# Low halves of the split numbers formed on VectorE, the cosine's whole turns taken on ScalarE, attention's outputs emptied at once, and the dense weights' conversion let in from head pair 5

## The chip, the cores and the metric

One core of one Trainium2 chip. The metric is the device time of one launch in microseconds (us); less is better. TensorE (PE) multiplies matrices, VectorE (DVE) and ScalarE (ACT) work elementwise from SBUF or PSUM, GpSimd (POOL) does so too and issues the indirect DMAs, SyncE (SP) issues the plain loads.

## What is computed

Three layers behind one another, all inputs and outputs in fp32.

```python
kv = einsum('bhsd,bhse->bhde', k, v); out = einsum('bhsd,bhde->bhse', q, kv)      # 8 x 8 x 576 x 64
x = out / sqrt(mean(out * out, -1) + 1e-6) * g_norm                               # -> x: 4608 x 512
logits = x @ w_gate                              # 8 experts, 576 tokens each, greedy by descending logit
out[tokens of e] = relu(x @ w1[e]) @ w2[e]       # 512 -> 1024 -> 512
h = out @ w_in; g = h * cos(h); result = g @ w_out      # 512 -> 2048 -> 512
```

## The kernel before

The two MLPs run in fp16 on TensorE, each number as a high half and a low half (`hi = fp16(x*s)`, `lo = fp16(x*s - hi)`), so that every product takes three matmuls (`mm3`).

**Attention** walks over 16 head pairs n (4 groups s of 4 pairs). For each, `kv_mm` forms k^T v in PSUM tile P, `kw_t` and `kw_mm` append the 8 gate columns, `tr` transposes q, and `o_mm` multiplies, in three parts g = 0, 1, 2, into PSUM tile pO (two buffers). pO holds groups of 64 output columns and 8 gate columns. `o_mm` empties it: ACT squares it (sq), ACT copies the 64-column blocks (xs), DVE copies the gate columns (LR) and sums the squares (SS). `norm(n)` runs for each pair and puts small DVE steps, one ACT square root and one POOL multiply (xs by R) on a list `late`, of which a few are issued at a time; after a group's last pair the rows go to DRAM (x_rows, from POOL's queue, 2304 KB a group). Loads of k, v, q run three pairs ahead on SP's queue.

**Conversion of the dense weights** (w_in, then w_out; `dense` and `dense_parts`) is background work in 8 parts of 4 units of 512 KB. A unit is loaded by SP into one of three io buffers, ACT rescales its high words (dG), and DVE merges it with three integer instructions into a staging tile (stA or stB, which alternate by part). Behind the fourth unit ACT takes the squares' sum of both tiles (junk), DVE and PE make the scale s (psm, psb, the matmul pq, peb, s), POOL multiplies each tile by s in place, ACT rounds it into the high half (win0 or wout0), and POOL subtracts into the low half. In attention this may run only after pair 13 (`if n > 13: side()`).

**Routing** (`Router.phase`, 8 phases) is a serial chain of small DVE steps and small matmuls (cmp, cn, nS, ...); phase 0 stands alone between attention and the MLPs, the others are woven in.

**Experts and the dense MLP** run over 16 units u of 288 tokens: h (w1), y (w2), then `yfin` (scale and split of y), o (the output product of the unit before, tiles of 128 tokens) and g (w_in with the cosine, `h2`). Weights of expert n are loaded by POOL's queue and split in `split_w` (expert 0 in `first_w`): ACT multiplies, ACT rounds, POOL subtracts. Unit 0's g may not start before the last part of w_in is converted (`flush("bg", ("in", 3))`) and unit 1's o not before the last part of w_out (`flush("bg", ("out", 3))`).

**The cosine** in `h2`, for 8 steps fp of 24 matmuls into one of three PSUM buffers ph: ACT writes r = p*s + 0.25 (et), DVE rounds it by adding and subtracting 1.5 * 2^23 (ek), DVE subtracts (et), ACT takes the sine (et), DVE multiplies by p (eg), ACT rounds (gT, first tile) and POOL subtracts (gT, second tile). The product of step fp is issued after the subtraction of step fp + 1, and the buffer ph is free after it.

The order on every engine is fixed when the kernel is built: `Meter` keeps a modelled clock for each engine, and `Sched` lets background jobs in where the modelled engine would be idle, by slack tables (`SLE`, `SLACK`, `PA`). So a changed cost also moves other instructions.

Of the kernel before, what the change touches and what calls it, by code (L numbers as in the profile page):

```python
# [19 lines left out]
E = 8  # L20
# [8 lines left out]
RB = 9  # L29
NHP = H // 2  # L30


def attention(nc, tc, q, k, v, w_gate, xrows, ident, gcol, L, M, sc):


    with ExitStack() as st:
# [5 lines left out]
        T = {}  # L42

# [19 lines left out]
        KV = [one.tile([128, 2, NHP, 2, D + E], F32, name=f"KV{i}") for i in range(2)]  # L63
# [3 lines left out]
        late = []  # L67
# [7 lines left out]
        def kv_of(n):  # L75

            return KV[n // NHP % 2][:, :, n % NHP]

        def kv_mm(n):
# [12 lines left out]
            for X in range(2):  # L92
                nc.scalar.activation(kv_of(n)[half[X], X, :, 0:D], P[half[X], :, 0:D], AF.Copy)
            for X in (1, 0):
                nc.vector.tensor_copy(kv_of(n)[half[1 - X], X, :, 0:D], P[half[X], :, 0:D])

        def kw_t(n):
            p = ps.tile([128, 4, 128], F32, name="pT", bufs=2)
            for X in range(2):
                for a in range(2):  # L100
                    nc.tensor.matmul(p[64 * a:64 * a + 64, X, 0:D], kv_of(n)[0:64, X, a, 0:D], ident[0:64, 0:64],
                                     start=True, stop=True)
            kvt[n] = wk.tile([128, 2, D], F32, name="kvt")
            nc.scalar.activation(kvt[n], p[:, 0:2, 0:D], AF.Copy)

        def kw_mm(n):
# [6 lines left out]
            nc.vector.tensor_copy(kv_of(n)[:, :, :, D:D + E], p[:, 0:2, 0:2 * E].rearrange("p x (a e) -> p x a e", a=2))  # L113
# [21 lines left out]
        def o_mm(n, g):  # L135
            s, hp = divmod(n, NHP)
            if hp == 0 and g == 0:
                XS[s] = wk.tile([128, RB, H, D], F32, name="xs", bufs=2)
# [4 lines left out]
            for j in range(J):  # L143
                for a in range(2):
                    o = (D + E) * (2 * j + a)
                    for X in range(2):
                        for i in range(N):
                            h = slice(64 * i, 64 * i + 64)
                            nc.tensor.matmul(pO[64 * X:64 * X + 64, i, o:o + D + E],
                                             qT[h, 2 * j + X, 64 * a:64 * a + 64], kv[h, X, a, :], start=True, stop=True)  # L150
            po = pO[:, 0:N, 0:2 * J * (D + E)].rearrange("p i (j a e) -> p i j a e", j=J, a=2)
            hs = slice(2 * hp, 2 * hp + 2)

            def rows(x):
                if g == 2:
                    return [x[:, 8, hs]]
                return [x[:, 4 * g + i:4 * g + 4:2, hs] for i in range(2)]

            sq = wk.tile([128, 2, 4, D], F32, name="sq", bufs=2)
            nc.scalar.activation(sq[:, 0:N, 0:2 * J], pO[:, 0:N, 0:2 * J * (D + E)].rearrange("p i (j e) -> p i j e", e=D + E)[:, :, :, 0:D], AF.Square)  # L160
            for i, x in enumerate(rows(XS[s])):
                nc.scalar.activation(x, po[:, i, 0, :, 0:D] if g == 2 else po[:, i, :, :, 0:D], AF.Copy)
# [7 lines left out]
            if g == 2:  # L170
                norm(n)

        def norm(n):
            s, hp = divmod(n, NHP)
            c, hs = slice(RB * s, RB * s + RB), slice(2 * hp, 2 * hp + 2)
            a = wk.tile([128, RB, 2], F32, name="na")
            y = wk.tile([128, RB, 2], F32, name="ny")
            w = wk.tile([128, RB, 2], F32, name="nw")
            x = XS[s][:, :, hs, :]

            def store():
                nc.gpsimd.dma_start(dview(xrows, 2 * s * S * DM, [[RB * DM, 128], [1, RB * DM]]),
                                    XS[s].rearrange("p r h e -> p (r h e)"))

            def logits():
                m = wk.tile([128, RB, H, E], F32, name="lm", bufs=1)
                nc.vector.tensor_mul(m, LR[s], R[:, c, :, None].to_broadcast([128, RB, H, E]))
                late.insert(0, lambda: nc.vector.tensor_reduce(L[:, c, :], m.rearrange("p r h e -> p r e h"), axis=AX,
                                                               op=OP.add))

            late.extend([
                lambda: nc.vector.tensor_scalar(a, SS[:, c, hs], 1.0 / D, 1e-6, op0=OP.mult, op1=OP.add),
# [15 lines left out]
        for n in range(NP + 1):  # L208
# [280 lines left out]
MF = 1.0  # L489
# [198 lines left out]
class Sched:  # L688
# [9 lines left out]
    def __init__(self, meter):  # L698
# [8 lines left out]
        self.held = None  # L707

# [74 lines left out]
    def step(self, name, force=False):  # L783
# [16 lines left out]
        if not force and (job.ready > now + self.early - MF * (name == "fin") or any(c[e] > now + self.slack[e] for e in job.need)):  # L800
# [51 lines left out]
class Moe:  # L852

    def __init__(self, nc, tc, pers, sm, C, xrows, w1, w2, w_in, w_out, out, gcol):
# [11 lines left out]
        nc.vector.memset(self.qtr, 0.25)  # L866
        self.win = [t([128, 4, FF], F16, f"win{i}") for i in range(2)]
        self.wout = [t([128, 16, DM], F16, f"wout{i}") for i in range(2)]
# [81 lines left out]
    def split_far(self, x, s, hi, lo):  # L950
# [613 lines left out]
```

## Time and profile before

| | |
|---|---|
| median of 3 runs | 1550.81 us (1546.31 to 1557.15) |
| profiled execution | 1557.92 us, its span 1556.1 us |
| mean granted TensorE clock | 0.927 of full |
| busy: PE, DVE, ACT, POOL | 88%, 54%, 43%, 37% of the span |

How to read it: a busy share is an average over stages with different limits, so the stages are looked at one by one: attention (0 to 145.4 us), routing phase 0 and the first gathers (to 202.6), the first h, y and h (to 268.2), the first g (to 306.3), y of unit 1 (to 323.8), a stretch with almost no matmul (to 359.7), o of unit 0 (to 389.8), and the rest to 1547.5. In a row of the timeline the last bracket is the idle time of the engine before the instruction and who ended it.

### The profile page before, as it was taken

The page shows a single profiled execution, that of the slowest core. Times are in us where ns is not written, and L with a number is a line of the kernel's source. Part 1 is how long each engine was busy: PE and PEld are TensorE (multiplying, and loading weights), DVE is VectorE, ACT ScalarE, POOL GpSimd, SP SyncE. Part 2 cuts the span into 40 slices and gives each one's busy share as a digit, 9 for nine tenths or more (in the row PEclk, how much of TensorE's full clock was granted, in tenths as well). Part 3 has the DMA queues.
Part 4 walks back from the last instruction along what each step waited for, and adds up shares of the span by engine and source line. Part 5 has one row for each costly group of instructions (what it writes and reads, how often), then busy time and mean ns, then how long its engine had stood idle before and what let it go on. Part 6 is the DMA issues. An engine that isn't in the chain of part 4 may idle for free.

```text
span 1556.1 us, 29014 instructions
## 1 busy us (share of the span) xinstructions
PE 1364.8 (88%) x12072; PEld 918.4 (59%) x12072; DVE 838.4 (54%) x2081; ACT 672.8 (43%) x1133; POOL 573.7 (37%) x493
## 2 busy tenths in 40 slices
PE   6775368726999889998999899999999999999997
PEld 5664236512667556474757466667675757576763
DVE  3567887974766576656655762434243415343441
ACT  3454364634734452055505650366066506642230
POOL 0333463476733342037403640256037203531121
PEclk8786569867999999999999989999999999999999
DMA  7784622322220220003100210021003000200000
GB/s 263 287 286 152 213 94 82 109 67 82 75 76 14 65 68 21 19 4 98 60 8 8 92 62 8 15 96 62 10 5 125 29 21 1 82 1 15 1 14 21
DMA packets 40371, 109.35 MB, mean 70 GB/s; under 512 B 4272, under 2 KB 12464, under 8 KB 39728
## 3 DMA queue, kind: packets, MB, share of 16 engines
q0 software_dynamic: 15744, 62.40, 11.7%
q1 hardware_dynamic: 23808, 45.09, 8.7%
q8 instruction: 94, 1.54, 0.4%
q14 instruction: 37, 0.30, 0.1%
q10 hardware_dynamic: 688, 0.02, 0.0%
HBM read 88.62 MB, written 18.87 MB: 69 GB/s over the span
## 4 chain that ended last, share of the span: by engine, by line
PE 64%; DVE 10%; ACT 5%; POOL 5%; issue 3%; DMA 1%; POOLq 0%; DVEq 0%; ACTq 0%
PE ph L666 61%; PE pr L666 2%; ACT w1s L666 1%; DVE eg L666 1%; POOL stB L666 1%; POOL w2s L666 1%; POOL stA L666 1%; ACT stA L666 1%; ACT et L666 1%; PE pq L666 1%; DVE stB L666 1%; DMA out_dram<-eg,idx 1%; ACT junk L666 1%; ACT xT L666 1%; DVE cmp L666 1%
## 5 line engine op out<-in xcount | busy, mean ns | idle before, releaser
L666 PE MATMUL ph<-wout,gT 128*128 128x512 f16 x1728 | 400.8, 385 | 10.6 <-ACT wout L666 4.5
L666 PE MATMUL ph<-yT,win 128*128 128x288 f16 x3072 | 392.2, 288 | 16.1 <-DVE eg L666 13.7
L666 PEld LDWEIGHTS <-win 128*128 128x128 f16 x3072 | 300.1, 98 | 103.5 <-issue 21.9
L666 PEld LDWEIGHTS <-gT 128*128 128x128 f16 x1728 | 163.2, 99 | 210.0 <-issue 22.2
L666 POOL TENSOR_TENSOR gT<-eg,gT 128x576 f16<-128x576 f32 (+2 forms) x192 | 182.0, 963 | 262.4 <-ACT gT L666 261.7
L666 ACT ACTIVATE et<-ph,qtr,us 128x576 f32<-128x576 f32 x128 | 106.2, 831 | 345.2 <-PE ph L666 315.0
L666 PE MATMUL ph<-xT,w1s 128*128 128x288 f16 x1536 | 206.8, 294 | 17.5 <-DVE hT L666 8.3
L666 PE MATMUL ph<-hT,w2s 128*128 128x288 f16 x1536 | 204.7, 289 | 0.0
L666 PEld LDWEIGHTS <-w1s 128*128 128x128 f16 x1536 | 150.2, 100 | 62.4 <-issue 10.5
L666 POOL DMA_INDIRECT out_dram<-eg,idx x36 | 36.1, 1002 | 402.5 <-DVE scT L666 190.9
L666 PEld LDWEIGHTS <-w2s 128*128 128x128 f16 x1536 | 147.4, 99 | 38.2 <-issue 0.7
L666 DVE TENSOR_SCALAR ek<-et 128x576 f32<-128x576 f32 x128 | 63.3, 494 | 151.9 <-ACT et L666 151.7
L666 DVE SCALAR_TENSOR_TENSOR eg<-ph,cG,et 128x576 f32<-128x576 f32 x128 | 103.9, 812 | 10.7 <-POOL gT L666 5.3
L666 DVE TENSOR_TENSOR eg<-ph,scT 128x512 f32<-128x512 f32 x36 | 24.9, 691 | 150.1 <-PE ph L666 128.9
L666 DVE TENSOR_TENSOR et<-et,ek 128x576 f32<-128x576 f32 x128 | 98.3, 768 | 4.4
L666 ACT ACTIVATE gT<-eg 128x576 f16<-128x576 f32 (+2 forms) x192 | 92.2, 512 | 14.5 <-DVE eg L666 13.9
L666 ACT ACTIVATE et<-et 128x576 f32<-128x576 f32 x128 | 86.3, 674 | 4.8 <-DVE et L666 4.2
L666 DVE SCALAR_TENSOR_TENSOR hT<-ph,hT 128x576 f16<-128x576 f32 x64 | 48.1, 755 | 67.3 <-ACT hT L666 67.1
L666 ACT ACTIVATE yT<-ph,sy 128x576 f16<-128x576 f32 x32 | 22.0, 737 | 138.8 <-DVE sy L666 138.8
L666 ACT ACTIVATE hT<-ph 128x576 f16<-128x576 f32 x64 | 41.0, 646 | 85.4 <-PE ph L666 85.4
L666 POOL TENSOR_TENSOR xs<-xs,R 128x1152 f32<-128x1152 f32 x16 | 36.1, 2254 | 112.0 <-DVE R L666 82.3
L666 DVE TENSOR_REDUCE amy<-ph 128x1 f32<-128x576 f32 x32 | 24.1, 755 | 56.7 <-PE ph L666 56.6
(216 smaller groups left out, 1626.3 us busy)
## 6 DMA issues: line engine op xcount, KB each, us to landing
kt<-in_k_dram SPq DMA_DIRECT2D x16, 576.0 KB, 4.8
vt<-in_v_dram SPq DMA_DIRECT2D x16, 576.0 KB, 6.9
qt<-in_q_dram SPq DMA_DIRECT2D x16, 576.0 KB, 7.4
x_rows<-xs POOLq DMA_DIRECT2D x4, 2304.0 KB, 9.9
io<-in_moe_w_in_dram SPq DMA_DIRECT2D x16, 512.0 KB, 4.8
io<-in_moe_w_out_dram SPq DMA_DIRECT2D x16, 512.0 KB, 3.6
out_dram<-eg,idx POOLq DMA_INDIRECT x36, 2.8
io<-x_rows,idx POOLq DMA_INDIRECT x35, 3.6
```

Source lines behind the costliest of these rows:

```text
L666: return f(*a, **kw)
```

## The change

Six things. (1) Attention: the layout of kv becomes gates, columns, columns, gates for a pair of heads, so that one ACT instruction takes 4 x 128 output columns and one DVE instruction all gates; sums of squares are one reduction; `norm` runs once for each group of 4 pairs; the stores of groups 1 and 2 wait for pair 13; group 1's rows lie in wout's space. (2) The dense conversion may be issued from pair 5 on, with loads granted one by one (`GRANT`). (3) Dense low halves: ACT rounds straight from the staging tile with the scale, DVE forms the low half; POOL does nothing. (4) The same for the experts' weights. (5) Cosine: ACT writes k = int32(p*s + 0.25), DVE forms r = p*s - k, ACT takes sin(2 pi r + pi/2); the low half of the result is formed on DVE. (6) Slacks in `SLE` are set anew.

```diff
+LOADED = 13
+GRANT = {5: 1, 7: 1, 9: 1, 11: 1, 12: 2, 13: 99}
...
+            sq = wk.tile([128, 4, 2, D], F32, name="sq", bufs=2)
+            sqv = sq[:, 0].rearrange("p a e -> p (a e)") if g == 2 else sq.rearrange("p (j i) a e -> p j i (a e)", i=2)
+            nc.scalar.activation(sqv, po[..., E:E + 2 * D], AF.Square)
+            nc.scalar.activation(rows(XS[s]), po[..., E:E + 2 * D], AF.Copy)
             later()
-            for i, x in enumerate(rows(LR[s])):
-                nc.vector.tensor_copy(x, po[:, i, 0, :, D:D + E] if g == 2 else po[:, i, :, :, D:D + E])
-            for i, x in enumerate(rows(SS[:, RB * s:RB * s + RB])):
-                y = sq[:, i, 0:2 * J].rearrange("p (j a) e -> p j a e", a=2)
-                nc.vector.tensor_reduce(x, y[:, 0] if g == 2 else y, axis=AX, op=OP.add)
+            nc.vector.tensor_copy(lrows(LR[s]), gates(po))
+            nc.vector.tensor_reduce(srows(SS[:, RB * s:RB * s + RB]), sq[:, 0] if g == 2 else sq, axis=AX, op=OP.add)
             later()
-            if g == 2:
-                norm(n)
+            if g == 2 and hp == NHP - 1:
+                norm(s)
...
+            M.grant += GRANT.get(n, 0)
             for f in steps:
                 f()
-                if n > 13:
+                if n == LOADED:
+                    while held:
+                        held.pop(0)()
+                    HOLD.clear()
+                if n > 4:
                     side()
...
-            if len(raw) == min(len(units), used + 3) or not self.far and nc.moved > sc.now() + FX:
+            if len(raw) == min(len(units), used + 3, self.grant):
                 return
...
         def low(lo, x, hi, t):
-            yield "gpsimd", 2.08, t
-            nc.gpsimd.tensor_sub(lo, x, hi)
+            yield "vector", 1.2, t
+            nc.vector.scalar_tensor_tensor(lo, x, s, hi, op0=OP.mult, op1=OP.subtract)
...
-            yield "gpsimd", 2.08, t
-            nc.gpsimd.tensor_scalar(x, x, s, None, op0=OP.mult)
-            yield "scalar", 0.95, nc.last
-            nc.scalar.activation(hi, x, AF.Copy)
+            yield "scalar", 1.04, t
+            nc.scalar.activation(hi, x, AF.Identity, scale=s)
...
-            yield from self.split_far(x, s[:, 0:1], hi, lo)
+            self.nc.scalar.activation(hi, x, AF.Identity, scale=s[:, 0:1])
+            yield "result"
+            self.nc.vector.scalar_tensor_tensor(lo, x, s[:, 0:1], hi, op0=OP.mult, op1=OP.subtract)
...
+            k = wk.tile([128, 2, U], I32, name="ek", bufs=1)
+            nc.scalar.activation(k, p, AF.Identity, bias=self.quarter[:, 0:1], scale=s(2))
+            if last:
+                sine(*last)
+            if done:
+                high(*done)
             r = wk.tile([128, 2, U], F32, name="et")
-            nc.scalar.activation(r, p, AF.Identity, bias=self.qtr[:, 0:1], scale=s(2))
-            k = wk.tile([128, 2, U], F32, name="ek", bufs=1)
-            V.tensor_scalar(k, r, MAGIC, MAGIC, op0=OP.add, op1=OP.subtract)
+            V.scalar_tensor_tensor(r, p, s(2), k, op0=OP.mult, op1=OP.subtract)
...
-    E0, E1, H, Y, O = ((2.2, 1.25, 3.24), (1.93, 1.88, 6.34), (0.9, 2.0, 15.0), (2, 4.86, 8.62), (2, 3.96, 20))
+    E0, E1, H, Y, O = ((3, 3, 3.24), (3, 3, 6.34), (3, 3, 15.0), (3, 4, 8.62), (3, 4, 20))
```

What the change moves in the fixed order is shown at three places.

VectorE behind y of unit 1, where the last parts of w_out are converted (dG, io and stB belong to a unit's merge; psm, psb, peb and s4 to a part's scale; numbers tell tiles apart). Before:

```order
L666 SCALAR_TENSOR_TENSOR stB_4516<-io_4504,stB_4516 128x512
L666 TENSOR_REDUCE psm_4537<-am_4382 128x1
L666 TENSOR_SCALAR psb_4539<-psm_4537 128x1
L666 TENSOR_SCALAR peb_4543<-pq_4541 128x1
L666 TENSOR_SCALAR stB_4517<-dG_4535 128x512
L666 TENSOR_SCALAR s4_105<-peb_4543 128x1
L666 SCALAR_TENSOR_TENSOR stB_4517<-dG_4535,stB_4517 128x512
L666 SCALAR_TENSOR_TENSOR stB_4517<-io_4513,stB_4517 128x512
```

Now:

```order
L689 TENSOR_SCALAR s4_106<-peb_4249 128x1
L689 SCALAR_TENSOR_TENSOR stB_4215<-io_4118,stB_4215 128x512
L689 TENSOR_SCALAR stB_4215<-dG_4220 128x512
L689 SCALAR_TENSOR_TENSOR stB_4215<-dG_4220,stB_4215 128x512
L689 SCALAR_TENSOR_TENSOR wout_104<-stA_3868,s4_106,wout_104 128x8x128
L689 SCALAR_TENSOR_TENSOR stB_4215<-io_4137,stB_4215 128x512
L689 TENSOR_SCALAR stB_4216<-dG_4256 128x512
L689 SCALAR_TENSOR_TENSOR wout_104<-stA_3869,s4_106,wout_104 128x8x128
```

Before, the scale of part 2 (s4) stands between the merges of part 3, and eight merges follow the end of y; now four do, and the two low halves of part 2 stand between them.

GpSimd at the same place. Before (a multiply in place, then the low half):

```order
L666 TENSOR_SCALAR stA_4380<-stA_4380,s4_105 128x1024
L666 TENSOR_SCALAR stA_4381<-stA_4381,s4_105 128x1024
L666 TENSOR_TENSOR wout1_103<-stA_4380,wout0_102 128x8x128
L666 TENSOR_TENSOR wout1_103<-stA_4381,wout0_102 128x8x128
L666 TENSOR_SCALAR stB_4516<-stB_4516,s4_105 128x1024
L666 TENSOR_SCALAR stB_4517<-stB_4517,s4_105 128x1024
L666 TENSOR_TENSOR wout1_103<-stB_4516,wout0_102 128x8x128
L666 TENSOR_TENSOR wout1_103<-stB_4517,wout0_102 128x8x128
```

Now, from attention's end to the loads of expert 1, it holds multiplies of attention's rows and DMA issues only:

```order
L689 TENSOR_TENSOR xs_1939<-xs_1939,R_148 128x9x128 x4
L689 DMA x_rows<-xs_1939 128x4608
L689 DMA sti_2899<-in_moe_w1_dram,wi_2894 128x1024
L689 DMA sti_2901<-in_moe_w1_dram,wi_2894 128x1024
L689 DMA sti_2903<-in_moe_w1_dram,wi_2894 128x1024
```

All elementwise work on weights has left GpSimd; the four multiplies of attention's last group now stand together at its end.

VectorE in the cosine, two steps of a later unit. Before:

```order
L666 TENSOR_SCALAR ek<-et 128x576
L666 TENSOR_TENSOR et<-et,ek 128x576
L666 SCALAR_TENSOR_TENSOR eg<-ph,cG,et 128x576
L666 CAST cn<-pr 32x60
L666 TENSOR_SCALAR ek<-et 128x576
L666 TENSOR_TENSOR et<-et,ek 128x576
```

Now:

```order
L689 SCALAR_TENSOR_TENSOR et<-ph,us,ek 128x576
L689 SCALAR_TENSOR_TENSOR eg<-ph,cG,et 128x576
L689 TENSOR_TENSOR gT_3313<-eg,gT_3312 128x2x192
L689 TENSOR_TENSOR gT_3313<-eg,gT_3312 128x2x96
L689 SCALAR_TENSOR_TENSOR et<-ph,us,ek 128x576
```

The rounding and its subtraction have become one instruction that reads PSUM, and the low half, in one or two pieces, stands behind the product.

## Rows read from the trace of the kernel before

**Rows 1.** Windows by stage: length, busy us PE, PEld, DVE, ACT, POOL (instructions), clock, DMA.

```profile
145.40:202.60 57.20, 15.43 (x350) 12.67 (x350) 48.13 (x132) 18.60 (x31) 28.06 (x19) 0.50 0.56 192
202.60:268.20 65.60, 49.33 (x357) 33.85 (x358) 49.77 (x102) 35.39 (x53) 27.93 (x12) 0.83 0.26 81
268.20:306.30 38.10, 27.44 (x219) 20.11 (x218) 36.08 (x63) 21.87 (x32) 17.45 (x9) 0.87 0.32 97
323.80:359.70 35.90, 0.53 (x4) 0.31 (x3) 21.34 (x50) 14.43 (x22) 25.50 (x10) 0.55 0.23 73
359.70:389.80 30.10, 26.79 (x155) 11.65 (x155) 16.68 (x63) 13.31 (x18) 17.49 (x14) 0.85 0.33 105
389.80:656.00 266.20, 251.34 (x1971) 162.42 (x1970) 175.21 (x450) 111.83 (x174) 100.40 (x96) 0.97 0.15 49
656.00:1513.30 857.30, 838.03 (x6032) 565.23 (x6031) 395.13 (x871) 374.53 (x573) 300.90 (x288) 0.99 0.11 37
```

**Rows 2.** Waits, 202.6 to 360 us: total, times, longest.

```profile
PE pq L666 <- DVE psb L666: 31.5, 5, 15.7
...
PE ph L666 <- DVE eg L666: 8.8, 1, 8.8
```

**Rows 3.** Timeline, 329 to 360 us: start, duration, engine, operation.

```profile
329.14 6.51 POOL L666 TENSOR_SCALAR stB<-stB,s 128x1024 f32<-128x1024 f32 x2 [5.47 <-DVE s L666]
...
335.62 4.38 POOL L666 TENSOR_TENSOR wout<-stB,wout 128x1024 f16<-128x1024 f32 x2
...
341.66 0.42 DVE L666 TENSOR_SCALAR stB<-dG 128x512 int32<-128x512 int32 x1
...
342.84 0.69 DVE L666 SCALAR_TENSOR_TENSOR stB<-io,stB 128x512 int32<-128x512 int32 x1
...
353.45 1.06 ACT L666 ACTIVATE junk<-stB 128x1024 bf16<-128x1024 f32 x1
...
358.63 1.06 ACT L666 ACTIVATE wout<-stB 128x1024 f16<-128x1024 f32 x1 [4.03 <-POOL stB L666]
359.74 0.58 PE L666 MATMUL ph<-wout,gT 128*128 128x512 f16 x1 [4.54 <-ACT wout L666]
```

**Rows 4.** Timeline in the first g, 274 to 282 us.

```profile
274.65 4.83 POOL L666 TENSOR_TENSOR win<-stB,win 128x1024 f16<-128x1024 f32 x2
...
277.54 2.49 DVE L666 SCALAR_TENSOR_TENSOR stA<-io,stA 128x512 int32<-128x512 int32 x1
...
281.06 1.55 ACT L666 ACTIVATE et<-ph,qtr,us 128x576 f32<-128x576 f32 x2 [4.71 <-issue]
```

**Rows 5.** Timeline, 195 to 210 us: two low halves of w1 on VectorE.

```profile
195.94 5.94 DVE L666 SCALAR_TENSOR_TENSOR w1s<-sti,sg,w1s 128x1024 f16<-128x1024 f32 x1 [1.33 <-ACT w1s L666]
196.56 4.23 POOL L666 TENSOR_TENSOR win<-stA,win 128x1024 f16<-128x1024 f32 x2
...
208.83 1.28 DVE L666 SCALAR_TENSOR_TENSOR w1s<-sti,sg,w1s 128x1024 f16<-128x1024 f32 x1
```

**Rows 6.** The page's groups of the cosine: count, busy us, mean ns, idle before.

```profile
L666 PE MATMUL ph<-yT,win 128*128 128x288 f16 x3072 | 392.2, 288 | 16.1 <-DVE eg L666 13.7
...
L666 ACT ACTIVATE et<-ph,qtr,us 128x576 f32<-128x576 f32 x128 | 106.2, 831 | 345.2 <-PE ph L666 315.0
...
L666 DVE TENSOR_SCALAR ek<-et 128x576 f32<-128x576 f32 x128 | 63.3, 494 | 151.9 <-ACT et L666 151.7
L666 DVE SCALAR_TENSOR_TENSOR eg<-ph,cG,et 128x576 f32<-128x576 f32 x128 | 103.9, 812 | 10.7 <-POOL gT L666 5.3
...
L666 DVE TENSOR_TENSOR et<-et,ek 128x576 f32<-128x576 f32 x128 | 98.3, 768 | 4.4
...
L666 DVE SCALAR_TENSOR_TENSOR hT<-ph,hT 128x576 f16<-128x576 f32 x64 | 48.1, 755 | 67.3 <-ACT hT L666 67.1
```

**Rows 7.** Groups of ScalarE in attention, 8 to 146 us, by form.

```profile
L666 ACT ACTIVATE xs<-pO 128x256 f32<-128x256 f32 x64 | 21.0, 385 | 0.0
L666 ACT ACTIVATE sq<-pO 128x512 f32<-128x512 f32 x32 | 19.1, 598 | 20.5 <-PE pO L666 20.3
```

More of the change, by code (lines that the diff above doesn't have):

```diff
@@ L62, in attention @@
             nc.vector.tensor_scalar(wgb[r, :, a, :], wgr[r], gcol[r], None, op0=OP.mult)
-        KV = [one.tile([128, 2, NHP, 2, D + E], F32, name=f"KV{i}") for i in range(2)]
+        W2 = 2 * (D + E)
+        KV = [one.tile([128, 2, NHP, W2], F32, name=f"KV{i}") for i in range(2)]
         SS = one.tile([128, NCOL, H], F32, name="SS")
@@ L66, in attention @@
         kvt, qTs, XS, LR = {}, {}, {}, {}
-        late = []
+        late, held = [], []
         M.prf = lambda: ps.tile([128, 4, 128], F32, name="pT", bufs=2).rearrange("p a b -> p (a b)")
@@ L152, in o_mm @@
             hs = slice(2 * hp, 2 * hp + 2)
-            def rows(x):
-                if g == 2:
[L156 to L162, printed above, removed]
@@ L181, in store, with norm, scaled @@
+            later()
+            if g == 2 and hp == NHP - 1:
+                norm(s)
+        def norm(s):
+            c = slice(RB * s, RB * s + RB)
+            a, y, w = (wk.tile([128, RB, H], F32, name=nm, bufs=1) for nm in ("na", "ny", "nw"))
+            x = XS[s]
+            m = LR[s]
+            def scaled(i):
+                h = slice(2 * i, 2 * i + 2)
+                nc.gpsimd.tensor_mul(x[:, :, h], x[:, :, h], R[:, c, h, None].to_broadcast([128, RB, 2, D]))
             def store():
@@ L182, in store @@
                 nc.gpsimd.dma_start(dview(xrows, 2 * s * S * DM, [[RB * DM, 128], [1, RB * DM]]),
[L183 to L189, printed above, removed]
+                                    x.rearrange("p r h e -> p (r h e)"))
@@ L799, in step @@
         c, now = self.m.clk, self.now()
-        if not force and (job.ready > now + self.early - MF * (name == "fin") or any(c[e] > now + self.slack[e] for e in job.need)):
+        if not force and (job.ready + self.margin.get(name, 0.0) > now + self.early - MF * (name == "fin") or any(c[e] > now + self.slack[e] for e in job.need)):
             return WAIT
@@ L865, in __init__ @@
         self.qtr = t([128, 1], F32, "qtr")
-        nc.vector.memset(self.qtr, 0.25)
+        nc.vector.memset(self.qtr, math.pi / 2)
+        self.quarter = t([128, 1], F32, "quarter")
+        nc.vector.memset(self.quarter, 0.25)
         self.win = [t([128, 4, FF], F16, f"win{i}") for i in range(2)]
-        self.wout = [t([128, 16, DM], F16, f"wout{i}") for i in range(2)]
+        self.wout2 = t([128, 2, 16, DM], F16, "wout")
+        self.wout = [self.wout2[:, i] for i in range(2)]
         self.s3 = t([128, 4], F32, "s3")
@@ L1312, in product, with views, high, low @@
             return g
-        def parts(fp, g):
+        def views(fp):
             for x0, x1, o in pieces:
-                hi, lo = (x[:, 2 * fp:2 * fp + 2, o:o + x1 - x0] for x in self.gT)
-                nc.scalar.activation(hi, g[:, :, x0:x1], AF.Copy)
-                nc.gpsimd.tensor_sub(lo, g[:, :, x0:x1], hi)
-        def sine(fp, r):
-            nc.scalar.activation(r, r, AF.Sin, scale=TURN)
+                yield (slice(x0, x1), *(x[:, 2 * fp:2 * fp + 2, o:o + x1 - x0] for x in self.gT))
+        def high(fp, g):
+            for c, hi, _ in views(fp):
+                nc.scalar.activation(hi, g[:, :, c], AF.Copy)
+        def low(fp, g):
+            for c, hi, lo in views(fp):
+                V.tensor_sub(lo, g[:, :, c], hi)
+        def sine(fp, p, r):
+            nc.scalar.activation(r, r, AF.Sin, bias=self.qtr[:, 0:1], scale=TURN)
         last = done = None
@@ L1334, in h2 @@
             p = ps[:, :, 0:U]
+            k = wk.tile([128, 2, U], I32, name="ek", bufs=1)
[4 more added lines that the diff above has]
+                high(*done)
             r = wk.tile([128, 2, U], F32, name="et")
[L1336 to L1338 removed]
+            V.scalar_tensor_tensor(r, p, s(2), k, op0=OP.mult, op1=OP.subtract)
+            new = None
             if last:
[L1340 removed]
+                new = last[0], product(*last)
             if done:
[L1342 to L1350 removed]
+                low(*done)
+            last, done = (fp, p, r), new
+            yield "G"
+        sine(*last)
+        high(*done)
+        g = product(*last)
+        low(*done)
+        high(7, g)
+        low(7, g)
     def tiles_of(self, u):
```

101 lines of the change are left out of this document (48 added, 53 removed).

## The prediction

> **What bounds the kernel now.** I first read the windows by stage [rows 1]. From 656 to 1513 us PE is busy 838.0 of 857.3 us at a clock of 0.99 of 2.4 GHz. There the matmuls are the bound, and at most some 20 us are to be had. From 389.8 to 656 it is 251.3 of 266.2. The loss lies before: in the 65.6 us of the first h, y and h PE is busy 49.3 us at 0.83, in the 38.1 us of the first g 27.4 at 0.87, and from 323.8 to 359.7 only 0.5 of 35.9. DVE is busy 49.8, 36.1 and 21.3 us there, so it is full in the first g (95%) and not in the other two. Then I read the waits of these stages [rows 2]: PE waited 31.5 us for psb, the step that makes a dense part's scale, and once 8.8 us for eg, the cosine's product. The timeline says why.
>
> Behind y of unit 1 the chain is the conversion of w_out [rows 3]. The scale is followed by 6.51 us of POOL for two multiplies, then ACT's rounding (1.06), then 4.38 us of POOL for two low halves; the staging tile comes free only then, and the next part's merges (0.42 + 0.69 + 0.69 = 1.80 us a unit) follow. PE starts o at 359.74, behind the rounding of the last part.
>
> In the first g DVE is held by POOL [rows 4]: while POOL forms two low halves of w_in (4.83 us), a merge step of DVE takes 2.49 us instead of 0.69 [rows 3, 4]. The scale for the cosine stands behind such steps in DVE's queue, ACT sits for 4.71 us, and PE's 8.8 us follow. At 195.94 the first low half of w1 takes 5.94 us beside two POOL low halves; the same instruction alone takes 1.28 [rows 5].
>
> **The change part by part.** The sum is made against the profiled execution, 1557.92 us; that is 7 us above the median of the runs, so I take the sum's difference and set it between the two.
>
> The stall before o of unit 0. In the new order four merges follow the end of y instead of eight, POOL has nothing, and two low halves stand between the merges. The path: about 1.5 us from the end of y to the scale of part 2 (small steps, an estimate), four merges 4 x 1.80 = 7.2, two low halves 2 x 1.28 = 2.6 [rows 5], the second pass over the squares 1.06 and its read-out, say 1.3 [rows 3], some 1.0 for total, matmul and scale, and the rounding 1.06: 14.7 us. Against 35.9 that is 21 us less. If the two low halves hide behind loads it is 24, if ACT's or the loads' order adds five, 16. I take 21.
>
> The first g. Win's low halves are formed on DVE before the first g begins, so the 2.49 us steps and the 8.8 us wait go. What DVE has in this g is 8 steps of its own (below, 2.42 each, 19.4) and conversion work for w_out of some 7 us: 26 of about 29. I take 9 us less; bounds 3 and 11. What is late next is DVE itself.
>
> The first h, y, h. Held DVE steps go, and win and the last quarter of w1 no longer pass through POOL; against that DVE gains low halves, 1.28 each, of which some six fall here (7.7 us) beside DVE's 49.8 of 65.6. ACT's conversion loses one pass of about 1.06 for each tile of w2 and w1 that was far. I take 4 us less; bounds 12 less and 5 more. O of unit 0 (30.1 us at 0.85 [rows 1]) starts after a shorter idle stretch; the clock's mean was 0.55 in the stall, nearly all at the 1.2 GHz level, and o began at it. I take 3 us less, bounds 0 and 7.
>
> Routing phase 0. The 5.94 us step becomes 1.28, which is 4.7 less in front of the first h; but POOL now has four multiplies of attention's last group in a row at its start, which I take at 2.4 us each, half of the 4.83 for two in [rows 4], and a DVE step with two SBUF operands may be held by one of them as in [rows 4]. That is +1.8 us a hit. I take 2 less for the first and 2 more for the second: 0, bounds 4 less and 6 more.
>
> Attention. For each full pO ACT does one copy of 512 columns for two of 256: from 2 x 0.385 to the square's 0.598 of the same width [rows 7], 0.17 us less, 32 times, 5.4 us if all of it is on the path. DVE has two instructions for four, and the norm runs 4 times instead of 16. Against that seven units of the conversion come in, with 1.80 us on DVE each (12.6 us) and a pass on ACT, into the idle time of both; seven loads of 512 KB stand in SP's queue between those of q, k and v, while two stores of 2304 KB are held back until pair 13. The norm of 72 columns at attention's end is longer by less than 1 us. I take 1 us less; bounds 8 less and 8 more.
>
> A page of the Trainium skill speaks against the merged copies: Perfetto Trace Analysis, section Optimizing Scalar/DVE Operations, says that where ScalarE and VectorE are not saturated but cause bubbles elsewhere, breaking instructions up may let work end sooner. By it the first half of a pO would be delivered 0.21 us later, 32 times, 7 us more, and the sum would be 36 in place of 43; but a pO is given back whole, so I keep the row.
>
> The cosine. DVE did 0.494 + 0.768 + 0.812 = 2.07 us a step [rows 6]; it will do r (from PSUM, with an int32 operand, which no row shows), the product 0.812, and the low half. For r the nearest rows are hT at 0.755 and eg at 0.812; I take 0.81. For the low half, one piece or two, hT's 0.755 and a fixed cost more: 0.80. That is 2.42 against PE's 24 x 392.2/3072 = 3.06 us. ACT's new k is as wide as the old et, 0.831; its bounds are 0.6 (512 columns without a scale, [rows 7]) and 0.9. The chain that gives ph back is k, r, product, 2.45 us, instead of et, ek, et, eg, 2.91. So nothing is added as long as DVE is not crowded. Cover: PE's 3.06; without it each 0.1 us a step above costs 12.8 us. I take 0, bounds 5 less and 12 more, and 1 us less at the end, where the last low half is on the path.
>
> The experts' weights. Eight low halves of 1.28 us for each expert go to DVE: 5.1 us a unit, with the cosine's 8 x 0.35 = 2.8 together 8 us in a unit of about 71. From 389.8 to 656 DVE is busy 175.2 of 266.2 (66%); with 8 x 266/71 = 30 more 77%, less the held steps. I take 4 us less there, bounds 14 less and 10 more; 0 after 656, where DVE is at 46%.
>
> The same section of that page says that where VectorE is saturated, moving work to ScalarE or GpSimd may pay, though the two share a port. Were DVE saturated, this change would go the wrong way; the 66% do not say so, and it is one of the rivals.
>
> The sum: 21 + 9 + 4 + 3 + 0 + 1 + 0 + 1 + 4 = 43 us less. From 1557.9 that is 1515, from the median 1508; I say **1511**.
>
> **The rivals.**
> A, the stall only moves. The planner puts merges earlier, and now they and the low halves crowd DVE in the first h and y and in attention, so that PE waits there. For it: DVE's 49.8 of 65.6 us, and 48.1 of 57.2 in routing phase 0 [rows 1]. Against: half of the crowding is held steps. Price: the bounds of three terms, +5, +8 and +6 instead of -4, -1 and 0, which is 24 us, and 5 more before o: 1540.
> B, more is won. With fewer gaps PE keeps the 2.4 GHz level from the first h to o of unit 0. The stages of 65.6, 38.1 and 30.1 us had 0.83, 0.87 and 0.85 [rows 1], so a third of their time was at 1.2 GHz, and half of that third, 20 us, was lost by it. Half of the 20, with the far bounds of the terms there (8, 2, 3 and 4 more), gives 27 us more: 1484.
> C, slower. The mechanism is DVE's step in the cosine. If r or the low half costs more than its neighbours, so that DVE's step passes PE's 3.06 us, all 128 steps are bound by DVE. It decides from +0.64 us a step. At 3.6 us (r and the low half at 1.4 each, three quarters above their rows) it is 0.54 x 128 = 69 us more: 1580. For it: the operands, int32 beside PSUM, and a low half in two pieces, are in no row. Against: all rows of 576 columns lie at 0.755 to 0.812.
> D, DVE is saturated by the units 1 to 6, by the rule above: 77% by average, and routing's chain waits behind low halves. If each of 6 units lost 5 us: 1541, much as in A; I count it there.
>
> **How the numbers follow.** Forecast, 1490 to 1530: 0.70. A with D, 1530 to 1555: 0.14. B, below 1490: 0.10. C: 0.06. A measurement of this kernel can tell about 1% (15.5 us) from no change. Faster than 1535: 0.70 + 0.10 + 0.05 of A = 0.85; slower by over 1%: 0.06; the same: 0.09. The range for 8 in 10 leaves half of B below and half of A and all of C above: 1484 to 1546.
>
> **What would show it.** Right: POOL's busy share falls from 37% to 10 to 14%, attention's multiplies and DMA issues alone; PE's gap before the first o of unit 0 is 12 to 20 us; no DVE merge above 1 us in the first g, and no wait of 8 us for eg there; r at 0.75 to 0.85 and the low half's pieces together below 0.9; attention ends between 137 and 153 us. Wrong: a PE stretch without matmuls of over 25 us between 200 and 350 us, PE waiting for eg in g of units 7 to 15, or attention ending later than 155 us. The saving should stand before 656 us; from there on the distance to the end should be the same within 12 us.

## The result, and the profile after

The kernel after takes 1460.3 us (median of three runs, 1459.3 to 1462.5): 0.9414 of the time before, with a 95% interval of 0.9371 to 0.9457. One disturbed run of it, 2008.3 us at a mean clock of 0.647, is left out. The profiled execution took 1462.46 us (span 1460.7, clock 0.950). That is 91 us less, where 40 were forecast, and below the range of 1484 to 1546.

The windows of the kernel after, cut at the same events as [rows 1] (y of unit 1, 291.9 to 304.8, is left out here as there); columns as there:

```profile
147.70:207.60 59.90, 16.21 (x360) 14.10 (x359) 47.62 (x127) 17.89 (x31) 22.86 (x16) 0.54 0.46 162
207.60:265.30 57.70, 45.82 (x349) 31.94 (x349) 50.74 (x116) 36.52 (x53) 3.18 (x2) 0.88 0.32 102
265.30:291.90 26.60, 25.74 (x220) 19.10 (x218) 23.14 (x45) 20.68 (x30) 0.00 (x0) 1.00 0.22 70
304.80:320.90 16.10, 0.34 (x3) 0.23 (x3) 12.92 (x30) 9.67 (x15) 0.00 (x0) 0.60 0.20 64
320.90:347.70 26.80, 25.63 (x156) 11.16 (x156) 19.94 (x71) 6.95 (x11) 7.40 (x8) 0.92 0.30 97
347.70:591.80 244.10, 242.97 (x1923) 158.61 (x1922) 169.36 (x447) 103.45 (x164) 35.15 (x42) 1.00 0.17 56
591.80:1418.00 826.20, 825.60 (x6098) 565.34 (x6097) 460.65 (x1005) 339.64 (x533) 87.89 (x108) 1.00 0.12 39
```

Read the first number of each row against its row of before, and then PE's share and the clock. The last two rows are the surprise: 266.2 to 244.1 and 857.3 to 826.2 us. PE's idle time there fell from 34.1 us to 1.7, and its busy time from 1089.4 to 1068.6 with the clock at 1.00. The same matmuls, without gaps, ran at the 2.4 GHz level throughout. Yet DVE is busier, 630.0 us for 570.3.

What PE waited for in these two stretches, before (389.8 to 1513 us) and after (347.7 to 1418): total, times, longest.

```profile
PE pr L666 <- DVE F L666: 9.3, 2, 6.3
PE pr L666 <- DVE Bm L666: 8.0, 3, 3.4
PE ph L666 <- DVE eg L666: 7.5, 6, 2.6
PE pr L666 <- DVE cmp L666: 5.2, 2, 4.0
PE pr L666 <- DVE cn L666: 1.5, 2, 1.2
```

```profile
PE ph L689 <- DVE eg L689: 1.1, 2, 0.8
PE pr L689 <- DVE cn L689: 0.5, 1, 0.5
```

Before, 24.0 us of the waits are for steps of routing (pr is its matmul); after, 0.5.

The page's groups of the cosine after (as [rows 6]):

```profile
L689 PE MATMUL ph<-yT,win 128*128 128x288 f16 x3072 | 384.2, 286 | 0.9 <-DVE eg L689 0.8
...
L689 ACT ACTIVATE ek<-ph,quarter,us 128x576 int32<-128x576 f32 x128 | 106.3, 830 | 327.1 <-PE ph L689 320.1
...
L689 DVE SCALAR_TENSOR_TENSOR et<-ph,us,ek 128x576 f32<-128x576 f32 x128 | 104.6, 817 | 135.5 <-ACT ek L689 135.2
...
L689 DVE SCALAR_TENSOR_TENSOR eg<-ph,cG,et 128x576 f32<-128x576 f32 x128 | 103.5, 809 | 2.7 <-ACT et L689 1.3
L689 DVE TENSOR_TENSOR gT<-eg,gT 128x576 f16<-128x576 f32 (+2 forms) x192 | 99.6, 550 | 0.7
```

k took 830 ns, r 817 and the low half 99.6/128 = 0.78 us a step: 2.40 us of DVE against the 2.42 that the sum used. So the instructions were priced well. What was not priced stands in the trace of before, at a place that I had not opened. Its timeline, 731.9 to 737 us, in a routing phase beside an o:

```profile
732.58 4.21 POOL L666 TENSOR_TENSOR w2s<-stB,w2s 128x1024 f16<-128x1024 f32 x2
732.67 2.08 DVE L666 TENSOR_SCALAR gt<-hi,at 128x36 f32<-128x36 f32 x1
...
734.73 2.09 DVE L666 TENSOR_SCALAR eq<-hi,at 128x36 f32<-128x36 f32 x1
736.74 0.24 DVE L666 SCALAR_TENSOR_TENSOR F<-mx,em,gt 128x36 bf16<-128x36 f32 x1
```

Each of GpSimd's two low halves, 2.1 us, holds one DVE step of 36 columns until it ends; alone these take 0.24 us. And the chain of work of before goes through them, to a wait of 3.1 us of PE:

```profile
732.67 2.08 DVE gt L666
...
734.81 2.01 DVE eq L666
...
737.26 0.32 PE pr L666
```

I compared every DVE step of before with the shortest of its own form, and counted those over 0.25 us longer that overlap a GpSimd multiply or subtraction: 53 steps, 70.3 us too long. Of these, 26 with 40.1 us lie between 389.8 and 1513 us, 21 of them in routing, and every wait of PE for routing of over 2 us there has such steps in its chain. In the kernel after there are 8, 12.8 us, and none behind 207.6 us.

### The profile page after: what moved, and what is told of

The parts are those of the page before. It is cut to its first block, busy times and chain, and to the rows that moved or that the text cites. A ratio compares the mean times of both kernels' runs of the same rounds, so it can differ in the third digit from the quotient of the medians.

```text
span 1460.7 us, 28545 instructions
## 1 busy us (share of the span) xinstructions
PE 1334.3 (91%) x12072; PEld 910.9 (62%) x12072; DVE 890.4 (61%) x2096; ACT 617.8 (42%) x1031; POOL 190.7 (13%) x211
## 4 chain that ended last, share of the span: by engine, by line
PE 77%; DVE 4%; ACT 2%; DMA 1%; issue 1%; POOL 0%; POOLq 0%; ACTq 0%; DVEq 0%; SPq 0%
PE ph L689 74%; PE pr L689 3%; PE pq L689 1%; DVE eg L689 1%; DVE stB L689 0%; ACT junk L689 0%; DMA sti<-in_moe_w_dram,wi 0%; DVE yT L689 0%; DMA io<-in_moe_w_out_dram 0%; DMA stB<-in_moe_w_dram,wi 0%; ACT ek L689 0%; DVE gT L689 0%; DVE stA L689 0%; ACT wout L689 0%; DVE wout L689 0%
## 5 line engine op out<-in xcount | busy, mean ns | idle before, releaser
L689 PE MATMUL ph<-wout,gT 128*128 128x512 f16 x1728 | 390.2, 380 | 5.0 <-DVE eg L689 2.6
L689 PE MATMUL ph<-yT,win 128*128 128x288 f16 x3072 | 384.2, 286 | 0.9 <-DVE eg L689 0.8
L689 ACT ACTIVATE ek<-ph,quarter,us 128x576 int32<-128x576 f32 x128 | 106.3, 830 | 327.1 <-PE ph L689 320.1
L689 PE MATMUL ph<-xT,w1s 128*128 128x288 f16 x1536 | 202.7, 291 | 9.3 <-DVE hT L689 6.4
L689 DVE SCALAR_TENSOR_TENSOR et<-ph,us,ek 128x576 f32<-128x576 f32 x128 | 104.6, 817 | 135.5 <-ACT ek L689 135.2
L689 PEld LDWEIGHTS <-w2s 128*128 128x128 f16 x1536 | 146.2, 98 | 36.3
L689 DVE TENSOR_TENSOR gT<-eg,gT 128x576 f16<-128x576 f32 (+2 forms) x192 | 99.6, 550 | 0.7
L689 ACT ACTIVATE et<-et,qtr 128x576 f32<-128x576 f32 x128 | 97.9, 765 | 0.6 <-DVE et L689 0.6
L689 POOL DMA_INDIRECT io<-x_rows,idx x35 | 34.2, 978 | 240.7 <-PE pq L689 198.5
L689 POOL DMA_INDIRECT stA<-in_moe_w_dram,wi x28 | 29.8, 1063 | 225.0 <-issue 187.8
L689 PE MATMUL pO<-KV,qTs 64*64 64x72 f32 x1152 | 41.0, 264 | 12.5 <-issue 9.9
```

The costliest lines, as they stand in the source:

```text
L689: return f(*a, **kw)
```

## The experiments

Theory H: GpSimd's elementwise work holds DVE's steps; DVE's chains run late; PE waits and loses its clock. Theory S: the shorter cosine chain gives ph back sooner. Theory W: the experts' weights are converted sooner. A fourth candidate is the new order of the instructions. In the runs that move work back to GpSimd, or put the old rounding back, the planner still counts the instruction of the kernel after, and another one is issued in its place (their diffs show what is issued); so PE's order, and the places on the other engines, are those of after throughout. All times are medians. "To after" is against 1460.3 us; the runs were made on several chips, on which the median of before lay between 1550.4 and 1553.4 us, so a few us there tell nothing. The ratio is to the kernel before on the same chip, with its interval.

| run | us | to after | ratio |
|---|---|---|---|
| cosine's low halves on GpSimd | 1468.1 | +7.8 | 0.9468 [0.9444, 0.9492] |
| experts' weights converted as before | 1498.1 | +37.8 | 0.9668 [0.9640, 0.9696] |
| added subtractions | 1552.8 | +92.5 | 1.0008 [0.9991, 1.0026] |
| added memsets | 1474.7 | +14.4 | 0.9511 [0.9484, 0.9539] |
| added copies | 1492.8 | +32.5 | 0.9618 [0.9573, 0.9663] |
| old rounding | 1473.3 | +13.0 | 0.9492 [0.9448, 0.9536] |
| low halves, weights, rounding together | 1521.3 | +61.0 | 0.9821 [0.9770, 0.9872] |
| w_in and w_out converted as before | 1495.9 | +35.6 | 0.9646 [0.9601, 0.9690] |
| no early units in attention | 1466.9 | +6.6 | 0.9458 [0.9431, 0.9485] |
| ten early units | 1454.2 | -6.1 | 0.9368 [0.9339, 0.9397] |
| last norm in two pieces | 1453.1 | -7.2 | 0.9364 [0.9338, 0.9390] |
| ten early units, norm in two | 1457.1 | -3.2 | 0.9387 [0.9361, 0.9414] |

**The low halves and the weights back on GpSimd.** The first two runs:

```diff
-                V.tensor_sub(lo, g[:, :, c], hi)
+                nc.gpsimd.tensor_sub(lo, g[:, :, c], hi)
```

> The kernel after, each engine's order unchanged, except that the low half of the cosine's product is formed on GpSimd again (same operands, same place in the order). After 389.8 us of the kernel before, the change won 53 us where I had put 4. Theory H (held steps): while GpSimd runs a two-operand subtraction, a VectorE step with two SBUF operands ends only with it (2.49 us for 0.69 in rows 4 and 3), so VectorE runs late, PE waits and falls to 1.2 GHz; with a third of GpSimd's elementwise work back, 8 to 25 us slower than after: 1469 to 1486. Theory S (shorter cosine chain: k, r, product in place of et, ek, et, eg gives ph back sooner): chain unchanged here, so within 5 us of after. Theory W (the experts' weights are converted in one ACT pass and one VectorE step, hence sooner): unchanged here, within 5 us of after.

```diff
-            self.nc.scalar.activation(hi, x, AF.Identity, scale=s[:, 0:1])
+            self.nc.scalar.activation(x, x, AF.Identity, scale=s[:, 0:1])
+            self.nc.scalar.activation(hi, x, AF.Copy)
...
-            self.nc.vector.scalar_tensor_tensor(lo, x, s[:, 0:1], hi, op0=OP.mult, op1=OP.subtract)
+            self.nc.gpsimd.tensor_sub(lo, x, hi)
```

> The kernel after, order unchanged, except that the conversion of the weights of experts 1 to 7 is the old one: two ACT passes and GpSimd's subtraction in place of one ACT pass and one VectorE step. H: these subtractions are the longest that GpSimd had, 2.2 us each, 56 of them; 15 to 45 us slower than after: 1476 to 1506. S: within 5 us of after. W: also slower, by 10 to 45 us, because the weights are late; what tells H from W is whether VectorE steps of 0.2 to 0.8 us become 1 to 2.4 us long beside GpSimd (H), or PE waits for w1s and w2s (W).

The first came out just under H's range, at +7.8. The second gave back +37.8. But GpSimd's result is waited for here, and the trace of the second run shows both theories at work. Behind 340 us, 13 DVE steps are held, 15.4 us in all, and PE waits 8.8 us for cmp, cn and Bm of routing (H); it also waits 8.0 us for psb, the scale of a loaded weight tile (W), and 14.6 us for eg. How the 37.8 us divide between them is open. The next run has GpSimd's work without anyone who waits for its result.

**Work that nobody waits for.** Behind each low half of the cosine and of a weight tile:

```diff
+        g.tensor_copy(self.idle[0:1, 976:977], hi)
+        g.tensor_sub(self.idle[:, 0:n], x, x)
```

> The kernel after complete, with GpSimd work added that nobody waits for: behind each low half of the cosine's product and of a weight tile of experts 1 to 7, GpSimd subtracts two constant fp32 operands of the same width into a scratch tile (paced by a one-element copy of the high half). H: VectorE's steps beside it are held although nothing depends on it; 15 to 50 us slower than after: 1476 to 1511. S and W: within 5 us of after, as both chains are untouched.

In the next run the second line is a memset, in the one after it a copy:

```diff
-        g.tensor_sub(self.idle[:, 0:n], x, x)
+        g.memset(self.idle[:, 0:n], 0.0)
```

> As the run with the added subtractions, but GpSimd only writes: a memset of the same scratch tile in the same places. H as SBUF State Buffer, section Who interferes with whom, of the Trainium skill words it (a VectorE instruction with two SBUF inputs contends with a GpSimd instruction that reads SBUF): no held steps, within 5 us of after. If GpSimd's mere presence, its issue slots or the one-element copies cost, as slow as the run with the subtractions.

```diff
-        g.tensor_sub(self.idle[:, 0:n], x, x)
+        g.tensor_copy(self.idle[:, 0:n], x)
```

> As the run with the added subtractions (1552.8 us), but GpSimd only copies one constant fp32 operand into the scratch tile: it reads SBUF, with one operand. If any GpSimd instruction that reads SBUF holds VectorE's steps with two SBUF operands: steps of VectorE are again as long as the copy beside them, and the run is 1500 to 1560, by how long the copies are. If it takes a GpSimd instruction with two operands: 1470 to 1480, as with the memset.

The added subtractions, whose result is never read, cost as much as the whole gain: +92.5 us, beyond H's range. S and W, whose instructions are untouched, cannot explain that. The same step, the low half of a w2 tile, in the timelines of the three runs (subtractions, memsets, copies):

```profile
700.57 2.94 DVE L689 SCALAR_TENSOR_TENSOR w2s<-stA,s,w2s 128x1024 f16<-128x1024 f32 x1
700.65 1.77 POOL L1130 TENSOR_TENSOR idle<-win 128x960 f16<-128x960 f32 x1
...
702.38 1.17 POOL L1128 COPY idle<-w2s 1x1 f16<-1x1 f16 x1
```

```profile
664.17 1.28 DVE L689 SCALAR_TENSOR_TENSOR w2s<-stA,s,w2s 128x1024 f16<-128x1024 f32 x1
664.25 0.89 POOL L1130 MEMSET idle<- 128x960 f16 x1
```

```profile
674.99 2.13 DVE L689 SCALAR_TENSOR_TENSOR w2s<-stA,s,w2s 128x1024 f16<-128x1024 f32 x1
675.06 0.98 POOL L1130 CAST idle<-win 128x960 f16<-128x960 f32 x1
```

Beside a subtraction of 1.77 us the step lasts 2.94, beside a copy of 0.98 it lasts 2.13, beside a memset of 0.89 it lasts 1.28, as alone: all but 0.1 us of GpSimd's length comes on top, and only where GpSimd reads. The medians over each whole run, from 260 us on, parted by whether one of the added instructions overlapped:

| DVE step | alone | subtraction | copy | memset |
|---|---|---|---|---|
| gT low half, 2x288, both operands in SBUF | 0.75 us | 1.56 | 1.27 | 0.75 |
| eg, product, one operand in PSUM | 0.81 us | 0.80 | 0.81 | 0.81 |

In the run with the subtractions DVE's low halves of the cosine's product cost 84.6 us more in all than in the kernel after (99.6 there):

```profile
L689 DVE TENSOR_TENSOR gT<-eg,gT 128x576 f16<-128x576 f32 (+2 forms) x192 | 184.2, 990 | 0.1
```

This is what the Trainium skill, SBUF — State Buffer, section Who interferes with whom, states: a VectorE instruction with two SBUF inputs contends with a GpSimd instruction that reads SBUF, not with one that only writes it. The runs agree in all three forms. The copies' 1492.8 us fell short of the 1500 that the expectation wanted at the least; they hold a step for 0.98 us where the subtractions hold it for 1.77, and a shorter hold may more often fit into DVE's slack (argued, not shown). The memsets still cost 14.4 us, 9 more than expected.

Not all of the 92.5 us need be steps held on PE's own path. GpSimd also issues the weight loads, in its own order, and these now stand behind the added work. In the run with the subtractions PE is idle for 64.4 us between 349.1 and 1505.6; three of its waits, 15.5 us (3.2, 6.3 and 6.0, at 723.59, 1055.19 and 1202.74), end a chain that runs from a weight load over ACT's squares of the loaded tile to the cosine's k, which stands behind them in ACT's order. In the run with the memsets PE waits once, 3.2 us, for psb. In the kernel before, two waits of 2.0 and 2.1 us (1068.80 and 1211.77) come by GpSimd's queue too: o's output is issued there behind low halves and weight loads, and DVE's next product waits for it to land. What this second path is worth alone was not tried.

**Old rounding, and all three together.**

```diff
-            nc.scalar.activation(k, p, AF.Identity, bias=self.quarter[:, 0:1], scale=s(2))
+            nc.scalar.activation(r, p, AF.Identity, bias=self.quarter[:, 0:1], scale=s(2))
...
-            V.scalar_tensor_tensor(r, p, s(2), k, op0=OP.mult, op1=OP.subtract)
+            v.tensor_scalar(k, r, MAGIC, MAGIC, op0=OP.add, op1=OP.subtract)
+            v.tensor_sub(r, r, k)
```

> The kernel after, order unchanged, with the cosine's old rounding: ACT writes et, VectorE rounds it into ek and subtracts, ACT's sine without bias; the low halves stay on VectorE and GpSimd does nothing of it. Theory S (a shorter chain to give ph back): the g stages of units 7 to 15, 23.5 us in the kernel after, go back to the 24.1 of before, 8 us in all, and 5 more in the first units: 1466 to 1480. H (held steps) alone: no GpSimd work, so no held steps; VectorE's step is 0.45 us longer (0.494 + 0.768 for 0.817), 57 us in all, still under PE's 3.06 a step: within 5 us of after.

> The kernel after, order unchanged, with all three at once: low halves of the cosine on GpSimd, the old conversion of the weights of experts 1 to 7, the old rounding. What I missed after 389.8 us of the kernel before was 53 us. If engines alone made it (H with S), this run gives it back: 7 (cosine's low halves) + 37 (weights) + 5 to 13 (rounding), 1500 to 1520. If the order of the instructions, which is that of after here, made a good part of it: under 1495. If the three aggravate each other (VectorE busier while it is held): over 1525.

The rounding is worth 13.0 us: S holds, as a small part. Each g from unit 7 on goes from 23.5 to between 24.0 and 24.2 us, with hardly a gap above 0.1 us: the matmuls seem to wait a little for ph each time. The three together gave +61.0, just above the expected 1500 to 1520 and near the sum of the single runs (7.8 + 37.8 + 13.0 = 58.6). Two windows of that run, 344.5 to 608.1 and on to 1474.3:

```profile
344.50:608.10 263.60, 249.82 (x1923) 160.52 (x1922) 158.07 (x415) 118.44 (x180) 104.83 (x98) 0.97 0.16 52
608.10:1474.30 866.20, 839.55 (x6098) 566.75 (x6097) 399.45 (x918) 376.35 (x573) 300.43 (x288) 0.99 0.11 37
```

Lengths, clocks and GpSimd's load are again those of the last two of [rows 1], but with the order of the kernel after: 1129.8 us for the 1123.5 of before and the 1070.3 of after. So with the old engines the new order wins nothing, and the 53 us come from the engines.

**The dense conversion back on GpSimd.**

```diff
-            nc.scalar.activation(hi, x, AF.Identity, scale=s)
+            nc.gpsimd.tensor_scalar(x, x, s, None, op0=OP.mult)
+            nc.scalar.activation(hi, x, AF.Copy)
...
-            nc.vector.scalar_tensor_tensor(lo, x, s, hi, op0=OP.mult, op1=OP.subtract)
+            nc.gpsimd.tensor_sub(lo, x, hi)
```

> The kernel after, order unchanged, with the conversion of w_in and w_out as before: GpSimd's multiply, ACT's rounding, GpSimd's subtraction. If the stall before o of unit 0 (16.1 us now, 35.9 before) and the first g (26.6 now, 38.1 before) were shortened by taking GpSimd out of the conversion: the stall is 26 to 36 us, the first g 30 to 38, and the run 1475 to 1500. If the earlier start of the conversion in attention did it: both stay within 4 us, and the run within 8 us of after.

```profile
279.70:316.00 36.30, 27.16 (x220) 19.84 (x218) 25.52 (x45) 22.70 (x32) 18.20 (x8) 0.95 0.20 61
328.90:352.50 23.60, 0.94 (x7) 0.56 (x6) 13.46 (x25) 9.44 (x14) 14.77 (x6) 0.56 0.15 45
381.80:626.00 244.20, 243.08 (x1924) 158.62 (x1923) 169.54 (x447) 103.57 (x164) 34.83 (x42) 1.00 0.17 56
```

The first g goes back to 36.3 us, as expected. But held steps are the smaller part of it: in this run's first g PE's waits of 5.2 and 2.3 us (291.09 and 315.98) end chains that start with GpSimd's two multiplies (6.03 and 5.68 us), for which ACT's rounding waits; behind it stand a merge and routing's steps in the first and the cosine's in the second. One held merge of 1.9 us lies in the first. The stall before o of unit 0 goes back to 23.6, less than expected, so 7.5 of its 19.8 us are GpSimd's absence; the early units (next) make 3.3 more, and the remainder was not separated. The rest of the run's cost lies before: attention ends 5.3 us later, at 153.0, routing phase 0 takes 2.6 us more and the first h, y and h 6.5. Behind o of unit 0 nothing changes. 35.6 here and 61.0 in the run before make 96.6, a little more than the whole gain of 91.

**When units are converted, and the norm.**

```diff
-GRANT = {5: 1, 7: 1, 9: 1, 11: 1, 12: 2, 13: 99}
+GRANT = {13: 99}
```

> The kernel after with no unit of the conversion of w_in released before head pair 13 (the planner orders the rest anew). If the early units are what shortens the stall and the first g: attention ends 3 to 6 us sooner (at 145 to 148 us, the 145.4 of before), seven units of 1.80 us of VectorE (12.6 us) come later, the stall before o of unit 0 is 22 to 30 us instead of 16.1, and the run is 1464 to 1480. If taking GpSimd out of the conversion is enough: the stall stays within 3 us and the run is 1455 to 1464.

Attention's last matmul ends at 145.2 us instead of 147.7; the stall is 19.4 us instead of 16.1. At 1466.9 us the early units are worth 6.6 by the medians (2.7 between the profiled executions). The stall lies between what the two theories wanted; the first g, 27.1 us, does without the early units.

```diff
+GRANT = {5: 1, 6: 1, 7: 1, 8: 1, 9: 1, 10: 1, 11: 1, 12: 2, 13: 99}
```

> The kernel after with three units more released in attention (one at each of the head pairs 5 to 11). If work moved ahead of the stall is won there: three units of 1.80 us on VectorE shorten the stall by 3 to 6 us, attention ends 1 to 3 us later: 1455 to 1463. If attention has no more room on VectorE: attention ends over 4 us later and the run is 1463 to 1470.

Faster by 6.1 us, but not as expected: the stall is gone whole (o follows y at once), not 3 to 6 us shorter, and attention's last matmul ends 7.2 us later, at 154.9.

```diff
+            cut = 3 if s == B // 2 - 1 else NHP
+            if g == 2 and hp == cut - 1:
+                norm(s, 0, cut)
+            elif g == 2 and hp == NHP - 1:
+                norm(s, cut, NHP)
```

> The kernel after with the norm of the last two batches done in two pieces: heads 0 to 5 after head pair 14, heads 6 and 7 at the end, so three of GpSimd's four multiplies of 2.1 to 2.6 us run before attention's end (the planner orders the rest anew). In the trace of after these four multiplies, 151.7 to 161.1 us, hold three VectorE steps of routing phase 0 (key 2.10 and 2.11, ti 1.79, alone 0.17 to 0.18): 5.5 us. Theory H: at most one hit is left, the distance from attention's end to the first h falls from 56.6 to 51 to 54 us, and the run is 1455 to 1460. If the three hits lie beside other work: within 2 us of after.

Timelines of routing phase 0, of the kernel after and then of this run:

```profile
151.66 9.40 POOL L689 TENSOR_TENSOR xs<-xs,R 128x1152 f32<-128x1152 f32 x4 [19.89 <-ACT dG L689]
...
154.53 2.10 DVE L689 TENSOR_SCALAR key<-m 128x36 int32<-128x36 int32 x1
...
156.92 2.11 DVE L689 TENSOR_TENSOR key<-key,m 128x36 int32<-128x36 int32 x1
...
159.32 1.79 DVE L689 TENSOR_SCALAR ti<-key 128x36 int32<-128x36 int32 x1
```

```profile
154.73 2.64 POOL L693 TENSOR_TENSOR xs<-xs,R 128x1152 f32<-128x1152 f32 x1 [0.39 <-DVE R L693]
...
157.60 0.17 DVE L693 TENSOR_SCALAR key<-m 128x36 int32<-128x36 int32 x1
...
158.09 0.19 DVE L693 TENSOR_TENSOR key<-key,m 128x36 int32<-128x36 int32 x1
...
158.57 0.17 DVE L693 TENSOR_SCALAR ti<-key 128x36 int32<-128x36 int32 x1
```

Three of the four multiplies now run before the key steps, and all three hits are gone. From attention's last matmul to the first h it is 56.0 us instead of 59.9; the expectation counted from 151.0 us, and the 3.9 lie within its 2.6 to 5.6. The h, y and h after it are 1.9 us shorter and the stall is 13.5; the planner ordered them anew, so what shortens them was not parted. At 1453.1 us this is the lowest median, though its runs (1452.3 to 1454.6) overlap those of the run before (1451.0 to 1455.6). The last run has the two edits above together.

> Both edits that made the kernel after faster, together: ten units of the conversion released in attention by pair 12 instead of seven, and the norm of the last two batches in two pieces. Alone they gave 1454.2 and 1453.1 us. If they are worth different things (the first moves work out of the stall before o of unit 0 and pays 7 us for it in attention, the second takes GpSimd's multiplies off routing phase 0): 1443 to 1450. If the first's longer attention crowds the second's room: 1450 to 1458.

The two do not add up: 1457.1, on a chip where before took 1553.4; its ratio is not clear of either single edit's. The stall is gone and the first h starts at 208.9 us, but the first h, y and h take 62.2 us for 57.7 and g of unit 1 takes 32.7 for 27.5. The work that left the stall seems to crowd the stages beside it; only the lengths show it.

## Why the prediction was wrong, point by point

| term | forecast | measured, us |
|---|---|---|
| attention | -1 | 145.4 to 147.7: +2.3 |
| routing phase 0 | 0 | 57.2 to 59.9: +2.7 |
| first h, y, h | -4 | 65.6 to 57.7: -7.9 |
| first g | -9 | 38.1 to 26.6: -11.5 |
| y of unit 1 | none | 17.5 to 12.9: -4.6 |
| stall before o of unit 0 | -21 | 35.9 to 16.1: -19.8 |
| o of unit 0 | -3 | 30.1 to 26.8: -3.3 |
| 389.8 to 656 | -4 | 266.2 to 244.1: -22.1 |
| 656 to 1513 | 0 | 857.3 to 826.2: -31.1 |
| end | -1 | -0.1 |

Up to the end of o of unit 0 the forecast was 38 less and 42.1 were measured. That these lie so close is partly luck: attention and routing phase 0 came out 6.0 us longer than their terms, and the first h, y and h, the first g and y 11.0 us shorter. The stall's path was worked out right (14.7 forecast, 16.1 measured). For the first g, GpSimd's absence was the right cause: it goes back to 36.3 us in the run with the dense conversion back on GpSimd. Of the held steps in [rows 4, 5] that run shows only a part there. Three hits of 1.6 to 1.9 us fell on routing phase 0, where I had allowed for about one.

**The step that failed** is "4 us less there, bounds 14 less and 10 more; 0 after 656, where DVE is at 46%". I priced GpSimd's absence stage by stage before 389.8 us; behind it I asked what eight low halves add to DVE's busy share, and put the held steps in as "less the held steps", without a price. The held steps do not need a full DVE. Most of them sit in routing's chain, where a step of 36 columns that takes 2.08 us instead of 0.24 delays everything behind it, and PE meets that delay in its own order (pr behind F). 26 held steps with 40.1 us lay behind 389.8 us; PE's idle time fell by 32.4 us when they went, and its busy time by 20.8. The single runs give 37.8 us for the weights' conversion (low halves and ACT's second pass), 13.0 for the rounding and 7.8 for the cosine's low halves; the new order added nothing. How much of the 37.8 is held steps, and how much is weights that come late, is open. My bound of 14 less was still 8 short.

Two more steps failed with it. "At most some 20 us are to be had" from 656 us on counted PE's idle time alone (857.3 - 838.0); 31.1 were won, 12.4 of them from PE's busy time, which fell from 838.0 to 825.6. Part of these is the clock, 0.99 to 1.00; part goes with the rounding, since in the run with the old rounding alone PE is busy for 832.5 us there, with the clock at 1.00. And the cosine's term took the shorter chain k, r, product as worth 0, with a bound of 5 less; putting the old rounding back costs 13.0.

**The rivals.** B (more is won, below 1490) is where the time came out, and partly for its cause: the clock rose from 0.83 to 0.88, 0.87 to 1.00 and 0.85 to 0.92 in its three stages, but more than half of the gain was later. A is seen in a small part: attention and routing phase 0 did get longer, 5.0 us of its 14, while its first h, y and h got shorter. C fell: r and the low half cost 0.817 and 0.78. D (DVE saturated by the units 1 to 6) fell too: DVE is busy 69% from 347.7 to 591.8 us, not 77%, and these units got shorter. Saturation was the wrong question; the shared port, which the sentence on the Trainium skill ahead of the sum names as well, was the right one. It speaks for this change, since it is the work on GpSimd that costs.

**What would show it.** POOL's share is 13%, PE's gap before o 16.1 us, the merges in the first g take 0.42 to 0.69, attention ended at 147.7: all right. The distance from 656 us to the end "the same within 12 us" was wrong: it fell by 31.2.

## What to carry to other kernels

Before pricing a move between VectorE and GpSimd, list every VectorE instruction that is longer than the shortest of its own form while a GpSimd multiply, subtraction or copy runs. Do that over the whole trace, and in serial chains first, whatever VectorE's busy share is. Look also at what stands behind GpSimd's work in its own queue. GpSimd work that nobody waits for is not free: here added subtractions cost 92 us, and added memsets 14.

## What was not expected of the hardware

GpSimd waits too: its copy of one element lasted 1.17 us beside a DVE low half of two SBUF operands in the run with the subtractions. In the run with the memsets it lasts up to 1.23 beside such a low half, and 0.18 with no DVE step beside it (391.60). A step with a single SBUF operand can be held as well: gt, a tensor_scalar, in the row at 732.67, and in the run with the memsets three copies of 4 fp32 columns, one of them here (1.00 us for 0.17; a one-element copy of GpSimd beside it ends at 977.94, the memset with the held step):

```profile
977.79 1.00 DVE L689 COPY scT<-sc 128x4 f32<-128x4 f32 x1
977.88 0.89 POOL L1130 MEMSET idle<- 128x960 f16 x1
```

So here a memset was not harmless to every form. The Trainium skill's section named above allows for that: it says that VectorE's 2-port modes, which copy and tensor_scalar can enter, contend with GpSimd too.
